# The second expert weight in two transfers, and the second product half by half of the inner units

## The chip, the cores and the metric

The kernel runs on one core of one Trainium2 chip. The metric is the device time of one execution in microseconds (us); lower is better. Engines are called as in the profile: PE (matmul), PEld (its weight loads), DVE (vector), ACT (scalar), POOL (which here issues the indexed transfers) and SP (which issues the plain ones).

## The reference

Four batches of 5056 tokens with 256 channels go through an attention over channels; its 20224 output rows go to one of 8 experts each. The core of it, shortened:

```
qn = q / (norm(q, axis=1) + 1e-6)          # q, k, v: 4 x 5056 x 256
kn = k / (norm(k, axis=1) + 1e-6)
a  = softmax(kn^T @ qn / tau)              # 4 x 256 x 256
x  = (v @ a).reshape(20224, 256)
e_idx  = argmax(x @ w_gate)                # one of 8 experts per row
gate_w = softmax(x @ w_gate)[e_idx];  eom = sigmoid(x @ w_output_gate)
for e in range(8):
    h  = relu(x[e_idx == e] @ w1[e])       # 256 -> 1024 inner units
    ye = h @ w2[e]                         # 1024 -> 256
    out[e_idx == e] = gate_w * eom[:, e] * ye
```

## The kernel before

**Stages.** The attention comes first: the products of k and q over all tokens (`gram`), then per batch v times a (`mix`), with the choice of the expert beside it (`route`), which scatters each token's row by expert into a buffer in DRAM, `xs_d`. The expert stage (`blocks`) starts while the last of that still runs, and fills the span from then on.

**Units.** The sorted tokens are worked off as 90 units. Units 0 to 53 have 256 tokens, that is two row tiles of 128 (`nt` is 2); from unit 54 on, units of 256 and of 128 tokens alternate. `FIRST` holds the first unit of each expert in the full part: 0, 7, 13, 20, 26, 33, 39 and 46.

**Numbers in two pieces.** x, h and both weights are kept as a sum of two fp16 numbers, hi and lo, and every product is three matmuls: hi by hi, hi by lo, lo by hi. `h_part` (L1011 to L1013) makes a quarter of the inner units, 12 matmuls, and ACT (L1015) and DVE (L1016) turn it into the hi and lo of `hb`. `y_part` (L1035 to L1037) makes a quarter of the second product. It has two row tiles t and two halves of the inner units fh, and takes tile 0 over the first half, tile 0 over the second, then tile 1 likewise: `t, fh = (part // 2, part % 2)`. ACT then scales y to `yo` (L1041), and POOL scatters `yo` to the output rows (L1048).

**Weights.** A weight is read as fp32 (`raw`), and `split` scales it by its size: ACT squares it (L348), DVE adds the sums up in `wtot` (L353), PE adds them over the partitions (`w_ps`, L354), and DVE takes the scale from it. Then ACT makes the hi (L369) and DVE the lo (L370), and SP writes both to `wsc` in DRAM (`keep`, L378). Each weight has two slots in SBUF, `wbuf`, and units take them in turn (`at_of`). Before a unit, POOL reads its weight from `wsc` into the slot (`fetch_w`, L904): 128 rows of 8 KB, found by an index per row from the table `wi`. Where the slot already holds that expert, the index lies out of bounds, and the transfer moves nothing. Units before the seventh use a weight that was split in place.

**x.** A unit's tokens come into `xg`, by POOL (L920) for units 20 to 68, else by SP. ACT (L985) and DVE (L986) make `xr` of them, hi and lo, and SP's transposing transfers (L990) turn this into `xt`. `xr` has two buffers, so that ACT waits with an `xr` for the transposes that still read the buffer.

**Order.** `blocks` writes iteration g as: fetch the first weight of the coming unit, the second weight of unit g, x some units ahead; store unit g-2; then four steps, each with a part of h of unit g and a part of y of unit g-1, and in between `prepare` for later x and the next steps of `split`. Each engine then works through its own list in a fixed order that a scheduler makes of this, by its own estimate of times; an instruction that waits holds up all that stands behind it on its engine. PE's list thus has h of a unit mixed with y of the one before, and now and then a `w_ps`. A transfer into a slot waits until PE has done with what the slot held: the first weight for h of two units before, the second for y of two units before.

## Time and profile before

| | |
|---|---|
| runs of the kernel | 1199.91, 1201.35 and 1203.97 us, median 1201.35 us |
| the profiled execution | 1198.02 us in all, of it 1196.3 us span |
| first matmuls on a fetched second weight | at 417 us |
| transfers issued by POOL | L904 into wbuf x166, L666 into xs_d x160, L1048 to the output x162, L920 into xg x49 |
| queue of POOL's transfers | 79.73 MB; its packets took 22.3% of the 16 DMA engines' span |
| queue of SP's transfers | 126.58 MB; 37.4% |

The profile is one execution, with times from the start of its span. In a timeline a row gives start, duration, engine, line, operation, tiles and, in brackets, the time for which the engine stood idle before it and what released it. A row of a group of instructions gives count, total busy time, mean ns of one, idle time before them and what ended most of it. A row of a window gives its length, then the busy time of PE, PEld, DVE, ACT and POOL with counts, the granted clock of PE, the busy share of the 16 DMA engines, and GB/s. "DMA wbuf<-wsc,wi" as a releaser means that a weight's transfer landed. In the names of tiles, `wbuf<-wsc,wi` stands for both weights.

### The profile page before, as it was taken

The page shows a single profiled execution, that of the slowest core. Times are in us where ns is not written, and L with a number is a line of the kernel's source. Part 1 is how long each engine was busy: PE and PEld are TensorE (multiplying, and loading weights), DVE is VectorE, ACT ScalarE, POOL GpSimd, SP SyncE. Part 2 cuts the span into 40 slices and gives each one's busy share as a digit, 9 for nine tenths or more (in the row PEclk, how much of TensorE's full clock was granted, in tenths as well). Part 3 has the DMA queues.
Part 4 walks back from the last instruction along what each step waited for, and adds up shares of the span by engine and source line. Part 5 has one row for each costly group of instructions (what it writes and reads, how often), then busy time and mean ns, then how long its engine had stood idle before and what let it go on. Part 6 is the DMA issues. An engine that isn't in the chain of part 4 may idle for free.

```text
span 1196.3 us, 27750 instructions
## 1 busy us (share of the span) xinstructions
PE 1170.8 (98%) x10412; PEld 1060.2 (89%) x10412; DVE 711.5 (59%) x2123; ACT 623.4 (52%) x1233; POOL 572.7 (48%) x561
## 2 busy tenths in 40 slices
PE   8999999999899999999999999999999999999998
PEld 7889899999788888888888888788889999999997
DVE  6666757658795755656565656554444555555551
ACT  5676757657745655546555555433333444444442
POOL 0004574757576334555544545444455644444443
PEclk9999999999999999999999999999999999999999
DMA  8986687857679964666655545732326442337643
GB/s 298 327 300 225 225 285 252 299 171 248 213 233 310 239 166 135 152 152 152 141 154 144 143 118 159 206 71 71 78 69 178 114 80 70 78 78 212 180 114 132
DMA packets 174882, 208.54 MB, mean 174 GB/s; under 512 B 120936, under 2 KB 124526, under 8 KB 169752
## 3 DMA queue, kind: packets, MB, share of 16 engines
q1 hardware_dynamic: 130312, 126.58, 37.4%
q0 software_dynamic: 43312, 79.73, 22.3%
q8 instruction: 84, 1.38, 0.5%
q10 hardware_dynamic: 1120, 0.42, 0.1%
q14 instruction: 54, 0.44, 0.1%
HBM read 275.55 MB, written 61.41 MB: 282 GB/s over the span
## 4 chain that ended last, share of the span: by engine, by line
PE 67%; issue 14%; POOL 8%; DMA 6%; ACT 2%; DVE 2%; SPq 1%; POOLq 0%; ACTq 0%; DVEq 0%
PE s_ps L444 9%; PE h_ps L1011 8%; PE h_ps L1013 8%; PE h_ps L1012 8%; PE y_ps L1037 8%; PE y_ps L1035 8%; PE y_ps L1036 8%; POOL out_dram L1048 4%; POOL wbuf L904 3%; PE x_ps L588 3%; PE x_ps L590 3%; PE x_ps L589 3%; PE vt_ps L558 2%; DMA qk<-in_k_dram 2%; DMA xt<-xr 1%
## 5 line engine op out<-in xcount | busy, mean ns | idle before, releaser
L1016 DVE SCALAR_TENSOR_TENSOR hb<-h_ps,hb 128x512 f16<-128x512 f32 (+1 forms) x360 | 228.0, 637 | 314.2 <-ACT hb L1015 314.0
L1015 ACT ACTIVATE hb<-h_ps 128x512 f16<-128x512 f32 (+1 forms) x360 | 197.2, 552 | 343.1 <-PE h_ps L1013 342.6
L1011 PE MATMUL h_ps<-xt,wbuf 128*128 128x256 f16 (+1 forms) x1440 | 366.6, 262 | 2.9 <-ACT st L591 2.9
L1013 PE MATMUL h_ps<-xt,wbuf 128*128 128x256 f16 (+1 forms) x1440 | 366.7, 262 | 0.0
L1012 PE MATMUL h_ps<-xt,wbuf 128*128 128x256 f16 (+1 forms) x1440 | 366.6, 262 | 0.0
L1035 PE MATMUL y_ps<-wbuf,hb 128*128 128x256 f16 x1296 | 353.3, 273 | 3.6 <-DMA wbuf<-wsc,wi 3.1
L1037 PE MATMUL y_ps<-wbuf,hb 128*128 128x256 f16 x1296 | 353.3, 273 | 0.3 <-DVE hb L1016 0.3
L1036 PE MATMUL y_ps<-wbuf,hb 128*128 128x256 f16 x1296 | 353.3, 273 | 0.0
L904 POOL DMA_INDIRECT wbuf<-wsc,wi x166 | 171.3, 1032 | 220.2 <-PE h_ps L1013 166.4
L666 POOL DMA_INDIRECT xs_d<-st,r_si x160 | 174.3, 1089 | 180.2 <-ACT st L591 96.1
L1048 POOL DMA_INDIRECT out_dram<-yo,b_id x162 | 169.9, 1049 | 64.4 <-issue 42.1
L1011 PEld LDWEIGHTS <-wbuf 128*128 128x128 f16 x1440 | 141.1, 98 | 15.7 <-issue 1.6
L1012 PEld LDWEIGHTS <-wbuf 128*128 128x128 f16 x1440 | 141.2, 98 | 15.3 <-issue 1.5
L444 PE MATMUL s_ps<-qk 128*128 128x256 f32 x640 | 149.4, 384 | 4.9 <-DMA qk<-in_q_dram 3.9
L1013 PEld LDWEIGHTS <-wbuf 128*128 128x128 f16 x1440 | 141.2, 98 | 13.5
L1036 PEld LDWEIGHTS <-hb 128*128 128x128 f16 x1296 | 126.8, 98 | 17.2 <-issue 3.4
L1037 PEld LDWEIGHTS <-hb 128*128 128x128 f16 x1296 | 126.8, 98 | 15.5 <-DVE hb L1016 0.8
L1035 PEld LDWEIGHTS <-hb 128*128 128x128 f16 x1296 | 126.8, 98 | 14.9 <-ACT hb L1015 1.1
L444 PEld LDWEIGHTS s_ps<-qk 128*128 128x128 f32 x640 | 119.0, 192 | 20.6 <-DMA qk<-in_k_dram 3.9
L920 POOL DMA_INDIRECT xg<-xs_d,gi x49 | 50.7, 1034 | 145.8 <-DVE xr L986 143.0
L406 DVE TENSOR_TENSOR acc<-acc,sq 128x1024 f32<-128x1024 f32 x76 | 93.1, 1225 | 45.8 <-ACT sq L405 39.9
L405 ACT ACTIVATE sq<-qk 128x1024 f32<-128x1024 f32 x76 | 80.4, 1060 | 53.3 <-DMA qk<-in_k_dram 47.3
(195 smaller groups left out, 1493.2 us busy)
## 6 DMA issues: line engine op xcount, KB each, us to landing
qk<-in_q_dram SPq DMA_DIRECT2D x75, 256.0 KB
qk<-in_k_dram SPq DMA_DIRECT2D x75, 256.0 KB
v<-in_v_dram SPq DMA_DIRECT2D x32, 512.0 KB
raw<-in_moe_w_dram SPq DMA_DIRECT2D x16, 1024.0 KB
xg<-xs_d SPq DMA_DIRECT2D x30, 272.0 KB
wsc<-whi SPq DMA_DIRECT2D x14, 512.0 KB
wsc<-wlo SPq DMA_DIRECT2D x14, 512.0 KB
v<-in_v_dram SPq DMA_DIRECT2D x8, 480.0 KB
```

Of the source, the lines that this page charges most:

```text
L444: nc.tensor.matmul(s_ps[:, c, :], kt[:, 1, t, c * P : (c + 1) * P], qt[:, 0, t, :], start=st == 0 and t0 == 0 and t == 0 and c == 0 and n ...
L666: ins = nc.gpsimd.indirect_dma_start(out=xs_d[:, :], out_offset=bass.IndirectOffsetOnAxis(ap=si[:np_, t : t + 1], axis=0), in_=st[:np_, t, ...
L904: nc.gpsimd.indirect_dma_start(out=wbuf[half][:, at_of(u), :], out_offset=None, in_=wsc[half][:end, :], in_offset=bass.IndirectOffsetOnAxi ...
L1011: nc.tensor.matmul(hp, w1s[:, 0, c, fs], xh, start=fi == 0 and c == 0, stop=False, **KWM)
L1012: nc.tensor.matmul(hp, w1s[:, 0, c, fs], xl, start=False, stop=False, **KWM)
L1013: main(PE=nc.tensor.matmul(hp, w1s[:, 1, c, fs], xh, start=False, stop=fin, **KWM))
L1015: main(ACT=nc.scalar.activation(hh, h_ps[:, :, :w], AF.Relu))
L1016: ins = nc.vector.scalar_tensor_tensor(out=hb[:, 1, 2 * fp : 2 * fp + 2, :w], in0=h_ps[:, :, :w], scalar=0.0, in1=hh, op0=ALU.max, op1=ALU ...
L1035: nc.tensor.matmul(y_ps[:, t, :], hb[:, 0, f, tsl], w2s[:, 0, f, :], start=st, stop=False, **KWM)
L1036: nc.tensor.matmul(y_ps[:, t, :], hb[:, 0, f, tsl], w2s[:, 1, f, :], start=False, stop=False, **KWM)
L1037: main(PE=nc.tensor.matmul(y_ps[:, t, :], hb[:, 1, f, tsl], w2s[:, 0, f, :], start=False, stop=fin, **KWM))
L1048: ins = nc.gpsimd.indirect_dma_start(out=out[:, :], out_offset=bass.IndirectOffsetOnAxis(ap=un["id"][:, t : t + 1], axis=0), in_=un["yo"][ ...
```

## The change

The second weight is laid out by halves of the inner units, in `wbuf` and in `wsc`: the half first, then hi and lo. It comes in two transfers of 128 rows of 4 KB, each with an index table of its own (`wi2`). `y_part` takes both row tiles over the first half (parts 0 and 1), then both over the second. The first half of the next unit's second weight is fetched after the second of the four steps of an iteration, the second half at the head of the next iteration, where the whole stood.

```diff
+    def by_pieces(a):
+        return a.rearrange("p (h a x) -> p h a x", h=2, a=2)
...
     def keep():
         with behind("SP"):
             for n, part in enumerate((hi, lo)):
-                nc.sync.dma_start(wsc[half][rows, n * HW1 : (n + 1) * HW1], part)
+                if half == 1:
+                    nc.sync.dma_start(by_pieces(wsc[1][rows, :])[:, :, n, :], part)
+                else:
+                    nc.sync.dma_start(wsc[half][rows, n * HW1 : (n + 1) * HW1], part)
...
+    wi2 = cst.tile([P, 2, NUNIT], I32, name="wi2")
...
         nc.vector.scalar_tensor_tensor(
-            out=wi[:, a:b], in0=ok, scalar=float(BIG), in1=row, op0=ALU.mult, op1=ALU.add
-        )
+            out=row, in0=ok, scalar=float(BIG), in1=row, op0=ALU.mult, op1=ALU.add
+        )
+        nc.vector.tensor_copy(wi[:, a:b], row)
+        for n in range(2):
+            nc.vector.tensor_scalar(
+                out=wi2[:, n, a:b], in0=row, scalar1=2.0, scalar2=float(n), op0=ALU.mult, op1=ALU.add
+            )
...
+    def fetch_w2(u, n):
+        if u < FIRST[1]:
+            return
+        end = 2 * (units[u]["top"] + 1) * P
+        nc.gpsimd.indirect_dma_start(
+            out=wbuf[1][:, at_of(u), 2 * n * (HW1 // 2) : 2 * (n + 1) * (HW1 // 2)],
+            out_offset=None,
+            in_=wsc[1].rearrange("r (n w) -> (r n) w", n=2)[:end, :],
+            in_offset=bass.IndirectOffsetOnAxis(ap=units[u]["wi2"][:, n, :], axis=0),
...
-        t, fh = (part // 2, part % 2) if nt == 2 else (0, part)
+        t, fh = (part % 2, part // 2) if nt == 2 else (0, part)
...
-            adv("w2", lambda u: fetch_w(1, u), g + NW - 1)
+            adv("w2a", lambda u: fetch_w2(u, 0), g + NW - 1)
+            adv("w2b", lambda u: fetch_w2(u, 1), g + NW - 1)
...
+                if fp == 1:
+                    adv("w2a", lambda u: fetch_w2(u, 0), g + NW)
```

In the engines' lists the first place is PE's, where unit 7's first y part begins (y of L1035 to L1037, h of L1011 to L1013; in the changed kernel these are L1069 to L1071 and L1044 to L1046). Before:

```order
L1013 MATMUL h_ps<-xt,wbuf_161 128x256
L1011 LDWEIGHTS wbuf_161
L1011 MATMUL h_ps<-xt,wbuf_161 128x256
L1035 LDWEIGHTS hb
L1035 MATMUL y_ps<-wbuf_162,hb 128x256
```

And in the changed kernel:

```order
L1045 MATMUL h_ps<-xt,wbuf_161 128x256
L1046 LDWEIGHTS wbuf_161
L1046 MATMUL h_ps<-xt,wbuf_161 128x256
L1069 LDWEIGHTS hb
L1069 MATMUL y_ps<-wbuf_162,hb 128x256
```

Before, y begins behind the first matmul of a triple, the seventh matmul of unit 8's second h part; now it begins behind the last of a triple, which ends the first h part, and is seven matmuls earlier in the list.

The second place is POOL's list among the units of two sizes (`wbuf_161` is the first weight, `wbuf_162` the second, `wi_169` the table `wi2`). Before, two units:

```order
L904 DMA wbuf_161<-wsc_85,wi 128x4096
L904 DMA wbuf_162<-wsc_86,wi 128x4096
L1048 DMA out_dram<-yo,b_id 20224x256 x2
L904 DMA wbuf_161<-wsc_85,wi 128x4096
L904 DMA wbuf_162<-wsc_86,wi 128x4096
L1048 DMA out_dram<-yo,b_id 20224x256
```

And in the changed kernel:

```order
L937 DMA wbuf_162<-wsc_86,wi_169 128x2048
L922 DMA wbuf_161<-wsc_85,wi 128x4096
L937 DMA wbuf_162<-wsc_86,wi_169 128x2048
L1082 DMA out_dram<-yo,b_id 20224x256
L937 DMA wbuf_162<-wsc_86,wi_169 128x2048
L922 DMA wbuf_161<-wsc_85,wi 128x4096
L937 DMA wbuf_162<-wsc_86,wi_169 128x2048
L1082 DMA out_dram<-yo,b_id 20224x256 x2
```

Per unit there is one transfer more, the first half of the second weight; it stands ahead of the next first weight, behind the stores.

The third place is on PE at a `w_ps` between units 28 and 29, here with the numbers of the buffers. Before (`y_ps_9389` is y of unit 27, `h_ps_9540` begins h of unit 29):

```order
L1037 LDWEIGHTS hb_9216
L1037 MATMUL y_ps_9389<-wbuf1_162,hb_9216 128x256
L354 LDWEIGHTS onesb_94
L354 MATMUL w_ps_9510<-wtot_9511,onesb_94 128x1
L1011 LDWEIGHTS wbuf0_161
L1011 MATMUL h_ps_9540<-xt_9129,wbuf0_161 128x256
```

And in the changed kernel (`y_ps_9631` is y of unit 28, `h_ps_9616` begins h of unit 29):

```order
L1069 LDWEIGHTS hb_9446
L1069 MATMUL y_ps_9631<-wbuf1_162,hb_9446 128x256
L363 LDWEIGHTS onesb_94
L363 MATMUL w_ps_9586<-wtot_9587,onesb_94 128x1
L1044 LDWEIGHTS wbuf0_161
L1044 MATMUL h_ps_9616<-xt_9199,wbuf0_161 128x256
```

`w_ps` now stands behind 22 matmuls of unit 28's y, which stood behind it before; the `w_ps` between units 34 and 35 has moved in the same way. On DVE nothing has moved at the `w_ps` behind unit 39: there, in both lists, two `xr`, two pieces of `hb` and then `wtot` follow each other, and on PE `w_ps` stands behind the same 22 matmuls of unit 39.

More of the change, by code (lines that the diff above doesn't have):

```diff
@@ L328, in split @@
         rows = slice(r * P, (r + 1) * P)
-        if r == 0:
+        if r == 0 and half == 1:
+            hi, lo = (by_pieces(wbuf[1][:, 0, :])[:, :, n, :] for n in range(2))
+        elif r == 0:
             hi, lo = (wbuf[half][:, 0, n * HW1 : (n + 1) * HW1] for n in range(2))
@@ L365, in split @@
         else:
-            src, dh, dl = raw, hi, lo
-            cuts = [(slice(None), slice(i * HW1 // 2, (i + 1) * HW1 // 2)) for i in range(2)]
+            src, dh, dl = raw.rearrange("p (h x) -> p h x", h=2), hi, lo
+            cuts = [(slice(None), i) for i in range(2)]
         for i, a in enumerate(cuts):
@@ L851, in add @@
                 units.append(
[L852 removed]
+                    dict(nt=nt, gi=gi[:, u : u + 1], wi=wi[:, u : u + 1], wi2=wi2[:, :, u : u + 1], top=max(r for r in range(E) if FIRST[r] <= u))
                 )
@@ L904, in fetch_w @@
         nc.gpsimd.indirect_dma_start(
-            out=wbuf[half][:, at_of(u), :],
+            out=wbuf[0][:, at_of(u), :],
             out_offset=None,
-            in_=wsc[half][:end, :],
+            in_=wsc[0][:end, :],
             in_offset=bass.IndirectOffsetOnAxis(ap=units[u]["wi"], axis=0),
+            bounds_check=end - 1,
+            oob_is_err=False,
+        )
[3 more added lines that the diff above has]
+        end = 2 * (units[u]["top"] + 1) * P
+        assert 2 * len(prepped) * P >= end
+        nc.gpsimd.indirect_dma_start(
[3 more added lines that the diff above has]
+            in_offset=bass.IndirectOffsetOnAxis(ap=units[u]["wi2"][:, n, :], axis=0),
             bounds_check=end - 1,
@@ L1034, in y_part @@
             fin = part == 3 and f == FC - 1
[L1035 to L1037 removed]
+            wh, wl = (w2s[:, a, f // (FC // 2), f % (FC // 2), :] for a in range(2))
+            nc.tensor.matmul(y_ps[:, t, :], hb[:, 0, f, tsl], wh, start=st, stop=False, **KWM)
+            nc.tensor.matmul(y_ps[:, t, :], hb[:, 0, f, tsl], wl, start=False, stop=False, **KWM)
+            main(PE=nc.tensor.matmul(y_ps[:, t, :], hb[:, 1, f, tsl], wh, start=False, stop=fin, **KWM))
         if part == 3:
```

17 lines of the change are left out of this document (8 added, 9 removed).

## The prediction

> **What bounds the kernel now.** First the page's head, to see which engine fills the span; then PE over the stretch in which the two products run; then PE's waits, which name all that can be won there.
>
> ```profile
> span 1196.3 us, 27750 instructions
> PE 1170.8 (98%) x10412; PEld 1060.2 (89%) x10412; DVE 711.5 (59%) x2123; ACT 623.4 (52%) x1233; POOL 572.7 (48%) x561
> PEclk9999999999999999999999999999999999999999
> ```
>
> PE is busy for 98% of the span, at the full granted clock in all 40 slices: no clock to win, and 25 us without work. One window takes in the units from the first fetched second weight on (span, then busy time of PE, PEld, DVE, ACT, POOL, clock, DMA share, GB/s); below it are PE's waits.
>
> ```profile
> 417.00:1176.00 759.00, 756.06 (x7324) 681.28 (x7324) 414.60 (x1259) 348.27 (x683) 366.85 (x355) 1.00 0.50 130
> ...
> PE y_ps L1035 <- DMA wbuf<-wsc,wi: 3.1, 2, 1.7
> PE w_ps L354 <- DVE wtot L353: 2.5, 3, 2.1
> PE y_ps L1035 <- ACT hb L1015: 0.5, 1, 0.5
> PE y_ps L1037 <- DVE hb L1016: 0.3, 1, 0.3
> ```
>
> In 759 us PE stands still for 759.00 - 756.06 = 2.94 us, and its matmul count does not change. In the whole span it waits for a second weight twice, 3.1 us together, once just ahead of this window and once in it. So the change cannot win much: first the ceiling, place by place. A wait is counted here as a gap beyond the cadence of matmuls, 0.11 us in the rows below (417.00 to 417.11 and so on).
>
> **Unit 7, the first weight wait** (PE's timeline; the number before the arrow is idle time; the windows as above; the last row is the piece of the chain that the load makes).
>
> ```profile
> 415.37 0.27 PE L1011 MATMUL h_ps<-xt,wbuf 128*128 128x256 f16 x1
> 417.00 0.27 PE L1035 MATMUL y_ps<-wbuf,hb 128*128 128x256 f16 x1 [1.36 <-DMA wbuf<-wsc,wi]
> 417.11 0.27 PE L1036 MATMUL y_ps<-wbuf,hb 128*128 128x256 f16 x1
> ...
> 412.00:414.50 2.50, 2.50 (x26) 2.24 (x24) 2.50 (x7) 2.50 (x3) 1.98 (x2) 1.00 1.14 397
> 414.50:417.00 2.50, 1.14 (x11) 0.88 (x9) 2.50 (x6) 1.34 (x4) 2.10 (x2) 1.00 0.71 263
> ...
> 408.50 8.46 DMA wbuf<-wsc,wi
> ```
>
> The next matmul would have been due at 415.37 + 0.11 = 415.48; it starts at 417.00, 1.52 us late. The load was issued at 408.50 and is in use 8.46 us later. Now two things change. The first half stands alone at the head of the queue, and the new order puts unit 7's first y part 7 matmuls earlier (before the second h part, where it stood in the middle of it), so PE asks at 415.48 - 7 x 0.11 = 414.71. When is half of the weight there? From 412.0 to 417.0 the DMA engines moved 2.5 x 397 + 2.5 x 263 = 1650 KB, of which the load's 128 rows of 8 KB are 1049 KB. If its packets went ahead of the others, 524 KB take 524/397 = 1.3 us, to 413.3; if all shared evenly, 825 KB take 2.1 us, to 414.1. I add up to 0.8 us until PE may use it, an estimate: by the same even pace the bytes end near 417. So 413.3 to 414.9, against 414.71: PE waits 0 to 0.2 us. **Term 1: -1.4 us**, bounds 0 (the half lands no earlier than the whole) and -1.52. The second half is asked for by the third part only, at least 36 matmuls (two parts of y and one of h, 3.9 us) after the first.
>
> A rule of the Trainium skill speaks against this, in "DMA: Bandwidth & Descriptors", section "Anatomy of one DMA — SWDGE (gpsimd) path": a transfer costs about 2.0 us that do not depend on its size, and bytes at 436 GB/s. By it the whole load would take 4.4 us and a half 3.2 us, estimates; the first half would come only 1.2 us sooner, at 415.8, and the term would be -0.4 us. The trace has 8.46 us for the whole, so the fixed part is not what sets it here.
>
> What gates the issue at 408.50 is the weight's way into DRAM: the load reads what SP writes here.
>
> ```profile
> 402.20 0.42 SPq L378 DMA_DIRECT2D wsc<-wlo  x1
> ```
>
> The change writes it in pieces of 2 KB instead of 4 KB (the wsc rows of the second weight are interleaved by halves). From 402.20 to 408.50 the write and the release take 6.3 us; no row has 2 KB pieces. If it gets 1.4 us slower, term 1 is gone; if faster, PE has nothing left to win. I take no change, the nearest row being this same write.
>
> **Unit 39, the second weight wait.** PE, then ACT and DVE, then the transfers ahead of them.
>
> ```profile
> 751.24 0.27 PE L1037 MATMUL y_ps<-wbuf,hb 128*128 128x256 f16 x1
> 753.23 0.27 PE L1035 MATMUL y_ps<-wbuf,hb 128*128 128x256 f16 x1 [1.72 <-DMA wbuf<-wsc,wi]
> 755.90 0.28 PE L1035 MATMUL y_ps<-wbuf,hb 128*128 128x256 f16 x1 [0.54 <-ACT hb L1015]
> 756.62 0.28 PE L1037 MATMUL y_ps<-wbuf,hb 128*128 128x256 f16 x1 [0.34 <-DVE hb L1016]
> 756.85 0.17 PE L354 MATMUL w_ps<-wtot,onesb 128*128 128x1 bf16 x1
> ...
> 754.46 0.91 ACT L985 ACTIVATE xr<-xg,b_sx 128x256 f16<-128x256 f32 x2 [6.24 <-DMA xt<-xr]
> ...
> 755.00 0.88 DVE L986 SCALAR_TENSOR_TENSOR xr<-xg,b_sx,xr 128x256 f16<-128x256 f32 x2 [6.05 <-ACT xr L985]
> 755.88 0.69 DVE L1016 SCALAR_TENSOR_TENSOR hb<-h_ps,hb 128x512 f16<-128x512 f32 x1
> 756.48 0.15 DVE L353 TENSOR_TENSOR wtot<-wss 128x1 bf16<-128x1 f32 x1
> ...
> 742.18 12.03 DMA xt<-xr
> ...
> 742.80 1.00 POOL L904 DMA_INDIRECT wbuf<-wsc,wi  x1 [0.30 <-issue]
> ```
>
> PE loses 753.23 - 751.35 = 1.88 us for the weight, then about 0.7 and 0.5 us for hb beyond the cadence: 3.1 us. The load was issued at 742.80. In the changed kernel its first half goes out as soon as unit 37's first two y parts are over, 24 matmuls and what lies between them sooner, so the weight will be there. But see what is late next. Behind 22 matmuls of unit 39 (12 + 10) stands w_ps, in both orders, and it reads wtot. wtot is DVE's third work behind xr, xr waits for ACT's xr, and ACT's xr waits for the transposes that end 742.18 + 12.03 = 754.21, because they still read the buffer that xr writes. Nothing of the change stands in that chain. So w_ps starts at 756.85 again, and PE, 22 x 0.11 = 2.4 us of matmuls after 751.35, waits for it from 753.8: the wait for the weight becomes a wait for wtot of about 3.0 us. **Term 2: -0.1 us.** Can the transposes land earlier? They share the DMA engines with the loads:
>
> ```profile
> 736.00:740.00 4.00, 4.00 (x40) 3.58 (x38) 3.84 (x14) 1.75 (x4) 2.00 (x2) 1.00 0.76 154
> 746.00:753.00 7.00, 5.51 (x51) 4.80 (x49) 2.55 (x11) 0.60 (x1) 0.44 (x1) 1.00 0.93 347
> ...
> 756.15 1.04 POOL L920 DMA_INDIRECT xg<-xs_d,gi  x1 [9.71 <-DVE xr L986]
> ```
>
> The first half of unit 39 moves out of the full stretch (0.93) into a freer one (0.76): 524 KB, at 347 GB/s 1.5 us less. But POOL is free for the 9.7 us before 756.15, and after unit 38's first two y parts the first half of unit 40 goes out in just that time and takes the room again. So I take no shift. Bounds: all 3.1 us won, if the transposes land 3 us earlier; 1.0 us lost, if the half of unit 40 holds them up by about as much (half of those 524 KB in their way).
>
> **The rest.** At two places w_ps waits for wtot by itself:
>
> ```profile
> 635.05 0.27 PE L1037 MATMUL y_ps<-wbuf,hb 128*128 128x256 f16 x1
> 635.49 0.18 PE L354 MATMUL w_ps<-wtot,onesb 128*128 128x1 bf16 x1 [0.17 <-DVE wtot L353]
> ...
> 698.83 0.18 PE L354 MATMUL w_ps<-wtot,onesb 128*128 128x1 bf16 x1 [0.17 <-DVE wtot L353]
> ...
> 365.69 0.18 PE L354 MATMUL w_ps<-wtot,onesb 128*128 128x1 bf16 x1 [2.14 <-DVE wtot L353]
> ...
> 364.84 0.69 DVE L1016 SCALAR_TENSOR_TENSOR hb<-h_ps,hb 128x512 f16<-128x512 f32 x1 [4.56 <-ACT hb L1015]
> ```
>
> 635.49 - 635.05 - 0.11 = 0.33 us each (the second like the first); the new order puts both 22 matmuls, 2.4 us, later on PE. **Term 3: -0.7 us**, bounds 0 and -0.7. At 365.69 three more matmuls stand ahead of w_ps (-0.3), but one yo of some 0.4 us stands ahead of hb on ACT, on whose end the DVE row waits (+0.4): **term 4: +0.1 us**, bounds -0.3 and +0.4. The added DVE work, three small operations in the weight tables, lies in the 4.56 us in which DVE waits for that hb: nothing; without that cover, about as much as three rows like wtot, 0.5 us.
>
> The price that recurs is POOL's:
>
> ```profile
> L904 POOL DMA_INDIRECT wbuf<-wsc,wi x166 | 171.3, 1032 | 220.2 <-PE h_ps L1013 166.4
> ...
> 1085.04 1.04 POOL L904 DMA_INDIRECT wbuf<-wsc,wi  x1 [3.56 <-PE h_ps L1013]
> 1092.30 1.01 POOL L904 DMA_INDIRECT wbuf<-wsc,wi  x1 [3.57 <-PE h_ps L1013]
> ...
> 1093.18 0.27 PE L1011 MATMUL h_ps<-xt,wbuf 128*128 128x256 f16 x1
> ```
>
> Half of 166, 83 more issues of 1.032 us, with 0.3 us between issues: some 110 us on POOL. Each goes out in the middle of a unit, when POOL waits anyway: 3.56 us ahead of the row at 1085.04, against 1.3 us. In POOL's order it stands ahead of the next xg and first weight, but what it waits for (the second y part) is over before what they wait for. Bytes are the same. **Nothing**; without this cover, see the slower rival. Sum: -1.4 - 0.1 - 0.7 + 0.1 = **-2.1 us**. The profiled execution took 1198.02 us (its span and 1.7 us around it), so 1195.9; the runs' median is 1201.35, 3.3 us above it, so 1199.3.
>
> **Rivals.**
> *Both weight waits vanish whole.* The transposes land 3 us earlier, wtot with them: -1.5 - 3.1 - 0.7 = -5.3 us, 1192.7 profiled, 1196.1 by the median (-0.44%). For it: the DMA engines are full until the weight lands, and what is ahead of the transposes gets less. Against: unit 40's half takes the room. Chance 0.2.
> *Slower: first weights land late among the pairs.* There the first weight goes out at 1085.04 and h uses it at 1093.18, 8.1 us later, while the loads above took 8.46 and 753.23 - 742.80 = 10.4 us. PE does not wait there now, so loads there are quicker or skipped. From the point at which a first weight lands more than 8.1 us after its issue, PE waits: 0.4 to 2.3 us by these two. Such loads come with a change of expert, seven changes times two slots, 14 at most; at half a microsecond each that is +7 us, 1205 profiled, 1208 by the median. For it: a third transfer shares the queue, and an issue of 1.3 us may stand ahead. Against: the half goes out sooner, and DMA is busy 0.50 of the window. Chance 0.1.
> *The halves are no sooner.* If the first half waits for all of the earlier y, or lands with the second, terms 1 and 2 are nothing, and 3 and 4 leave -0.6: 1197.4 profiled, 1200.8. For it: the release is seen on no row of before. Chance 0.1.
>
> **How the numbers follow.** Forecast 0.6, rivals 0.2, 0.1, 0.1. A measurement of this kernel tells apart some 0.3%, 3.6 us. Forecast and third rival lie inside, of the first rival most lies beyond, and single runs spread from 1199.91 to 1203.97, so I say faster 0.22, same 0.67, slower 0.11. The range has to reach the first rival, 1196.1 with 1 us for spread, and on the other side the bounds of terms 1, 2 and 4 (0, +1.0, +0.4: 1202.8 with no term 3): 1195.0 to 1203.3; the slower rival stays out.
>
> **What will show it.** Right: no wait of y for wbuf near 415; near 753 the same hole, but ahead of w_ps, put down to wtot, w_ps within 0.5 us of 756.85 less what was won before; no wait at the w_ps of 635 and 699; POOL busy for some 85 us more, PE as long as before. Wrong: y still waiting for wbuf (the halves land late), h waiting for wbuf between 900 and 1176 (slower rival), or transposes that end a microsecond or more earlier (first rival).

## The result, and the profile after

The changed kernel is **slower**, by 1.4%. Beside each other on one chip, its median is 1221.92 us (six runs, 1210.05 to 1223.93) and that of the kernel before 1202.66 us (six runs, 1197.74 to 1214.76): a ratio of 1.0142, with a 95% interval of 1.0103 to 1.018. The prediction said 1199.3 us, in a range from 1195.0 to 1203.3. The profiled execution took 1220.71 us, of it 1219.0 us span, which is 22.7 us more than the span before.

The head of the page after, then two lines of PE's waits (waited for: us in total, times, longest):

```profile
span 1219.0 us, 28028 instructions
PE 1176.1 (96%) x10412; PEld 1065.0 (87%) x10412; DVE 715.3 (59%) x2129; ACT 624.0 (51%) x1233; POOL 660.4 (54%) x644
PEclk9999999999899999999999999899999999999998
```

```profile
PE w_ps L363 <- DVE wtot L362: 10.4, 3, 9.8
PE y_ps L1069 <- DMA wbuf<-wsc,wi: 3.1, 1, 3.1
```

The matmuls are the same in number. POOL is busy for 660.4 - 572.7 = 87.7 us more with 83 more transfers, as forecast (85). Three slices show a granted clock below 0.9: around 305 to 335 us, where unit 0 begins, at unit 39 and at the end (a 9 stands for 0.9 or more, so it doesn't say that the clock was full). Where a weight was waited for twice, it is now waited for once, for as long; and a wait for `wtot` of 9.8 us has come up. These waits are not 22.7 us, so the rest has to be looked for where the waits of PE don't reach. Placing the same matmuls of the two timelines side by side, unit by unit, gives this ledger:

| stretch | lost (us) | forecast (us) |
|---|---|---|
| up to unit 6 | 2.1 | +0.1 (the `w_ps` of 365.69 us) |
| unit 7, first half of its weight | 3.1 | -1.4 |
| the two `w_ps` of 635 and 699 us | -0.8 | -0.7 |
| unit 39 | 8.3 | -0.1 |
| behind the last matmul | 9.95 | none |
| sum | 22.7 | -2.1 |

**Up to unit 6.** Of the 2.1 us, 1.55 stand ahead of unit 0's first matmul. Then the profiles part twice, by PE's clock. Both have a hole ahead of unit 0, of 3.12 us after and 2.94 before; behind it PE works at 0.50 after and at 1.00 before, and 2.4 us are lost. At the first `w_ps` that waited for `wtot` (365.69 us before) it is the other way round: before, 3.41 us at 0.50 follow the wait of 2.14 us; after, the waits there are 1.00 (for `hb`) and 0.40 us and the clock stays full, so that 2.2 us are won. By the next `w_ps` 0.4 are lost again. The windows, after and then before:

```profile
328.50:334.20 5.70, 5.69 (x34) 4.84 (x34) 2.33 (x9) 2.47 (x9) 4.20 (x5) 0.50 0.29 104
```

```profile
327.00:329.40 2.40, 2.40 (x22) 2.27 (x21) 1.15 (x7) 1.88 (x8) 1.79 (x3) 1.00 0.28 101
366.39:369.80 3.41, 3.41 (x19) 2.43 (x17) 2.20 (x3) 3.41 (x4) 2.54 (x3) 0.50 1.07 264
```

**The end.** The stretch from the last matmul to the end of the span, in windows, after and then before (length, busy time of PE, PEld, DVE, ACT, POOL, clock, DMA share, GB/s):

```profile
1203.40:1219.00 15.60, 0.00 (x0) 0.00 (x0) 0.00 (x0) 0.47 (x1) 1.40 (x2) 0.65 0.04 14
```

```profile
1190.60:1196.30 5.70, 0.04 (x1) 0.00 (x0) 0.00 (x0) 0.47 (x1) 1.44 (x2) 0.96 0.12 41
```

Nothing works in it, and what stands there issues no work, so neither busy times nor waits name it. The view of one source line names it: the last instructions of POOL's own sequencer (shortest/median/longest in ns, then the first and the last start in us). After and before:

```profile
L1178 POOLq INC_SWDGE_SEM  x1: 2071/2071/2071, 1208.3 to 1208.3; - x1
...
L1205 POOLq DRAIN  x3: 51/103/7745, 1210.4 to 1218.7; - x3
```

```profile
L1141 POOLq INC_SWDGE_SEM  x1: 411/411/411, 1194.1 to 1194.1; - x1
...
L1168 POOLq DRAIN  x3: 51/103/967, 1194.5 to 1196.0; - x3
```

One drain takes 7.745 us instead of 0.967, and the instruction ahead of it 2.071 instead of 0.411: 6.78 + 1.66 = 8.4 of the 9.95 us. The first stands at the test whether a rest of units is left, the second at the program's end; neither does work of the kernel. The other 1.5 us stand ahead of both: the first of them starts 4.9 us behind the last matmul instead of 3.4. They vary by themselves: in five other profiles with the same count of transfers and all halves early, or all but one (`e1_again`, `e3_head`, `e9_but40`, `e15_but39`, `e18_change`) the end takes 13.75 us or 13.76 instead of 15.62.

**Unit 39.** In order, each from its own view after: PE's timeline, ACT's, DVE's, the piece of the chain of waits that the transposes make, and POOL's issues ahead of and during them.

```profile
768.11 0.18 PE L363 MATMUL w_ps<-wtot,onesb 128*128 128x1 bf16 x1 [9.79 <-DVE wtot L362]
...
768.38 0.42 PE L1045 MATMUL h_ps<-xt,wbuf 128*128 128x256 f16 x1
768.59 0.42 PE L1046 MATMUL h_ps<-xt,wbuf 128*128 128x256 f16 x1
```

```profile
765.88 0.91 ACT L1018 ACTIVATE xr<-xg,b_sx 128x256 f16<-128x256 f32 x2 [13.25 <-DMA xt<-xr]
...
767.90 0.15 DVE L362 TENSOR_TENSOR wtot<-wss 128x1 bf16<-128x1 f32 x1
```

```profile
746.60 19.02 DMA xt<-xr
```

```profile
742.13 1.02 POOL L937 DMA_INDIRECT wbuf<-wsc,wi  x1 [0.30 <-issue]
...
745.68 1.00 POOL L922 DMA_INDIRECT wbuf<-wsc,wi  x1 [0.30 <-PE y_ps L1071]
746.99 1.00 POOL L937 DMA_INDIRECT wbuf<-wsc,wi  x1 [0.30 <-PE h_ps L1046]
...
750.96 1.03 POOL L937 DMA_INDIRECT wbuf<-wsc,wi  x1 [0.33 <-PE y_ps L1071]
```

The chain is the one that the prediction followed, from the transposes over ACT's `xr` and DVE's `xr` and `hb` to `wtot` and `w_ps`. Only its first link has another length: 19.02 us where it had 12.03. The four issues are unit 39's first half, unit 40's first weight, unit 39's second half and unit 40's first half. Windows of the trace after show what the transposes met (first over all of their 19.02 us, then a part of them), and what the hole did to PE's clock; below, apart, is the window over the transposes before:

```profile
746.60:765.62 19.02, 11.72 (x108) 10.27 (x105) 3.76 (x12) 1.79 (x3) 4.14 (x5) 0.88 0.92 211
752.00:754.00 2.00, 2.00 (x20) 1.80 (x19) 1.14 (x4) 0.60 (x1) 0.00 (x0) 1.00 0.17 59
758.30:768.10 9.80, 0.02 (x1) 0.00 (x0) 1.64 (x4) 2.12 (x5) 0.53 (x1) 0.63 0.54 164
768.20:771.10 2.90, 2.90 (x15) 2.09 (x16) 1.58 (x5) 2.32 (x3) 2.29 (x3) 0.50 1.21 172
```

```profile
742.18:754.21 12.03, 10.31 (x95) 9.10 (x93) 3.62 (x12) 1.79 (x3) 3.35 (x4) 1.00 0.88 282
```

While the transposes ran, 19.02 x 211 = 4013 KB were moved, against 12.03 x 282 = 3392 KB before. The 621 KB more account for 2.2 us at 282 GB/s; the other 4.8 of the 7.0 us are a lower rate, and in the part from 752 to 754 the engines moved just 59 GB/s, with transposes still to land. The packets of the trace show what stood there: fourteen of POOL's, of 4352 bytes each, the size in which x comes into `xg` (64 of them are a unit's 272 KB), began between 748.87 and 750.99, took 2.1 to 5.7 us and ended between 753.1 and 754.5; ten more (nine of x, one of a first weight) began from 754.01 on and ended together at 757.4. The median packet of x takes 0.2 us in this stretch. In the last window, behind the hole, PE works at 0.50 of its clock: a matmul every 0.21 us (768.38, 768.59) instead of 0.11, which is 14 matmuls by 0.1 = 1.4 us. With the 7.0 us by which the transposes take longer, that makes the 8.3 within a tenth.

**Unit 7.** PE's timeline after, the load's piece of the chain, and windows before and behind the hole:

```profile
420.05 0.37 PE L1069 MATMUL y_ps<-wbuf,hb 128*128 128x256 f16 x1 [3.07 <-DMA wbuf<-wsc,wi]
```

```profile
408.91 11.10 DMA wbuf<-wsc,wi
```

```profile
416.00:418.00 2.00, 0.98 (x9) 0.72 (x8) 2.00 (x5) 1.95 (x5) 1.69 (x2) 1.00 1.03 168
...
420.00:421.00 1.00, 0.95 (x5) 0.69 (x5) 0.55 (x2) 0.83 (x2) 0.19 (x1) 0.50 1.04 362
421.00:422.00 1.00, 1.00 (x7) 0.67 (x6) 0.59 (x2) 0.07 (x1) 1.00 (x1) 0.50 0.51 190
```

Half the weight took 11.10 us, where the whole had taken 8.46. PE begins y 420.05 - 417.00 = 3.05 us later than before, of which 2.1 were lost earlier; it has then done 7 matmuls of h less (0.8), and 14 or so matmuls run at half the clock (1.4): 3.1 us in all.

### The profile page after: what moved, and what is told of

Its sections match the earlier page's. It is cut to its first block, busy times and chain, and to the rows that moved or that the text cites. A ratio compares the mean times of both kernels' runs of the same rounds, so it can differ in the third digit from the quotient of the medians.

```text
span 1219.0 us, 28028 instructions
## 1 busy us (share of the span) xinstructions
PE 1176.1 (96%) x10412; PEld 1065.0 (87%) x10412; DVE 715.3 (59%) x2129; ACT 624.0 (51%) x1233; POOL 660.4 (54%) x644
## 3 DMA queue, kind: packets, MB, share of 16 engines
q8 instruction: 84, 1.38, 0.5%
## 4 chain that ended last, share of the span: by engine, by line
PE 83%; DMA 7%; issue 3%; ACT 2%; POOL 2%; DVE 1%; POOLq 0%; SPq 0%; ACTq 0%; DVEq 0%
PE h_ps L1044 10%; PE h_ps L1045 10%; PE h_ps L1046 10%; PE y_ps L1069 10%; PE y_ps L1071 10%; PE y_ps L1070 10%; PE s_ps L456 9%; PE x_ps L600 3%; PE x_ps L602 3%; PE x_ps L601 3%; PE vt_ps L570 2%; DMA xt<-xr 2%; DMA qk<-in_k_dram 2%; POOL xs_d L678 1%; DMA xs_d<-st,r_si 1%
## 5 line engine op out<-in xcount | busy, mean ns | idle before, releaser
L1044 PE MATMUL h_ps<-xt,wbuf 128*128 128x256 f16 (+1 forms) x1440 | 367.3, 263 | 3.1 <-ACT st L603 3.1
L1046 PE MATMUL h_ps<-xt,wbuf 128*128 128x256 f16 (+1 forms) x1440 | 367.1, 263 | 0.0
L1069 PE MATMUL y_ps<-wbuf,hb 128*128 128x256 f16 x1296 | 353.8, 273 | 4.1 <-DMA wbuf<-wsc,wi 3.1
L1071 PE MATMUL y_ps<-wbuf,hb 128*128 128x256 f16 x1296 | 353.9, 273 | 0.0
L678 POOL DMA_INDIRECT xs_d<-st,r_si x160 | 177.1, 1107 | 178.7 <-ACT st L603 97.6
L937 POOL DMA_INDIRECT wbuf<-wsc,wi x166 | 172.2, 1037 | 89.8 <-PE y_ps L1071 58.3
L1044 PEld LDWEIGHTS <-wbuf 128*128 128x128 f16 x1440 | 141.3, 98 | 16.3 <-DMA xt<-xr 1.9
L1046 PEld LDWEIGHTS <-wbuf 128*128 128x128 f16 x1440 | 141.4, 98 | 13.6
L922 POOL DMA_INDIRECT wbuf<-wsc,wi x83 | 85.0, 1024 | 106.7 <-PE h_ps L1046 96.6
L1069 PEld LDWEIGHTS <-hb 128*128 128x128 f16 x1296 | 127.0, 98 | 15.3 <-ACT hb L1048 1.3
L1071 PEld LDWEIGHTS <-hb 128*128 128x128 f16 x1296 | 127.0, 98 | 15.1 <-DVE hb L1049 0.2
```

The source lines that it names most:

```text
L678: ins = nc.gpsimd.indirect_dma_start(out=xs_d[:, :], out_offset=bass.IndirectOffsetOnAxis(ap=si[:np_, t : t + 1], axis=0), in_=st[:np_, t, ...
L937: nc.gpsimd.indirect_dma_start(out=wbuf[1][:, at_of(u), 2 * n * (HW1 // 2) : 2 * (n + 1) * (HW1 // 2)], out_offset=None, in_=wsc[1].rearra ...
L1044: nc.tensor.matmul(hp, w1s[:, 0, c, fs], xh, start=fi == 0 and c == 0, stop=False, **KWM)
L1046: main(PE=nc.tensor.matmul(hp, w1s[:, 1, c, fs], xh, start=False, stop=fin, **KWM))
L1069: nc.tensor.matmul(y_ps[:, t, :], hb[:, 0, f, tsl], wh, start=st, stop=False, **KWM)
L1071: main(PE=nc.tensor.matmul(y_ps[:, t, :], hb[:, 1, f, tsl], wh, start=False, stop=fin, **KWM))
```

## The experiments

Two theories stood against each other. **Places:** the halves, sent out earlier, meet the transposes, and the two holes are the loss. **Count:** 83 more transfers cost by themselves, at the end or between. Ratios are to the kernel before on the same chip. The chips differ: before took 1203 to 1205 us on the chip of the result and on that of `e5` to `e8`, but 1285 to 1294 us on the four others, where PE loses, in the profiles taken there, many small waits that the profile puts to "issue", with no releaser. So most verdicts below rest on a place in the trace, not on the total.

### Which part is it: the order, the early half, or the count?

**The change once more**, on another chip.

> The changed kernel once more, unchanged. Theory A (the early half of unit 40's weight runs beside the transposes and holds them up): the same picture, w_ps behind unit 39 waits 8 to 11 us for wtot, the transposes of about 747 take 17 to 20 us, ratio to before 1.010 to 1.018. Theory D (the long transposes and the long end were an accident of one execution): the wait falls to 3 us or the end stretch (last matmul to end of span, 15.9 us against 5.9 before) to 6 us, and single times spread by over 8 us.

1317.55 against 1294.4 us, ratio 1.020 (1.0138 to 1.0262). PE's timeline and the transposes in the chain:

```profile
844.99 0.19 PE L363 MATMUL w_ps<-wtot,onesb 128*128 128x1 bf16 x1 [10.93 <-DVE wtot L362]
```

```profile
825.01 17.48 DMA xt<-xr
```

The wait of unit 39 and the long transposes come again on a chip that is slower throughout. Unit 7 waits 1.9 us here.

**The new order of y alone**, in the kernel before.

```diff
-        t, fh = (part // 2, part % 2) if nt == 2 else (0, part)
+        t, fh = (part % 2, part // 2) if nt == 2 else (0, part)
```

> The kernel before with the new order of y's parts alone: both row tiles over the first half of the inner units, then over the second; the second weight whole as before. Theories A and B (issue count): nothing changes, ratio 0.997 to 1.003, the first weight wait still 1.4 us, w_ps at 757. Theory C (the order itself costs): slower by 0.5% or more, with y waiting for hb somewhere.

1299.4 us, ratio 1.0037 (1.0003 to 1.0072). PE waits 4.0 us for unit 39's weight, nowhere long for `wtot`, and the end stretch is 5.56 us. The order is not the loss.

**Both halves called at the head of the iteration**, nothing after the second step.

```diff
-                if fp == 1:
-                    adv("w2a", lambda u: fetch_w2(u, 0), g + NW)
```

> The changed kernel with both halves fetched at the head of the iteration, nothing early: as many issues as the change, bytes of unit 40 no longer beside the transposes. Theory A: the transposes near 745 take 12 us again, w_ps behind unit 39 waits 3 us or less, -8 us against the change; if the long end comes from the number of issues (theory B) it stays at 14 to 16 us and the ratio to before is about 1.008; if not, 1.000 to 1.003. Theory B alone (more transfers as such slow the transposes): w_ps waits 8 us or more here too, ratio 1.010 to 1.018.

1315.54 us, ratio 1.0159 (1.0099 to 1.022). The scheduler brought POOL's transfers into the same order as in the change, the first halves early, so this undid nothing: `w_ps` waits 9.5 us and the end takes 13.75 us, as with the change. It is a third profile of that order. Where a call stands in the code does not say where the transfer goes.

**83 empty transfers in the kernel before**: all their indices lie out of bounds, so each costs an issue and moves nothing.

```diff
+                if fp == 1 and FIRST[1] <= g + 1 < min(len(units), z):
+                    none_i = sm.tile([P, 1], I32, tag="none_i", name="none_i")
+                    nc.vector.tensor_scalar(
+                        out=none_i, in0=units[g]["id"][:, 0:1], scalar1=0.0, scalar2=float(BIG), op0=ALU.mult, op1=ALU.add
+                    )
+                    nc.gpsimd.indirect_dma_start(
+                        out=none_o[:, :],
...
```

> The kernel before with one more indexed transfer per unit from unit 7 on, all of its indices out of bounds, so that it moves nothing, in POOL's list where the change has the first half (and one small DVE operation for its index). Theory B: the end stretch grows to 14 to 16 us and the ratio is 1.006 or more; if the transposes suffer from the number of transfers too, 1.010 or more. Theory A: the middle stays as before, w_ps behind unit 39 near 757 with no wait beyond 3 us; ratio 0.998 to 1.004 if the long end isn't from the count of issues.

1341.18 us, ratio 1.038 (1.0306 to 1.0455). There is no long wait for `wtot` (the longest is 0.6 us), but the end takes 14.06 us, with the drain at 7745 ns to the nanosecond of the change. So the count alone brings the end; the halves are not needed for it. PE's "issue" waits add up to 66 us, against 43 to 54 in the three runs above, so the total is no measure of the price.

### The parts apart, on a chip as fast as that of the result

**Both halves late**, one right behind the other at the head of the iteration.

```diff
+    def fetch_both(u):
+        b = fetch_w2(u, 1)
+        if b is not None:
+            with tc.issue_after(b.ins):
+                fetch_w2(u, 0)
...
-            adv("w2a", lambda u: fetch_w2(u, 0), g + NW - 1)
-            adv("w2b", lambda u: fetch_w2(u, 1), g + NW - 1)
+            adv("w2", fetch_both, g + NW - 1)
...
-                if fp == 1:
-                    adv("w2a", lambda u: fetch_w2(u, 0), g + NW)
```

> The changed kernel with both halves issued next to each other, the second half and then the first, when the whole of the earlier y is over: as many transfers as the change, but no half of unit 40 before the w_ps behind unit 39. Theory A (unit 40's early half, beside the transposes, makes them long): transposes 10 to 13 us at that place, w_ps waits 0 to 3 us for wtot; end stretch 14 to 16 us as in the change, ratio to before about 1.007. Rival (any second weight in two transfers of 4 KB rows makes them long): w_ps waits 8 us or more again, ratio 1.012 or more.

1208.04 against 1204.67 us, ratio 1.0051 (1.0009 to 1.0093). PE's timeline at unit 39, the transposes, and the end:

```profile
752.26 0.27 PE L1075 MATMUL y_ps<-wbuf,hb 128*128 128x256 f16 x1 [0.57 <-DMA wbuf<-wsc,wi]
...
755.63 0.18 PE L363 MATMUL w_ps<-wtot,onesb 128*128 128x1 bf16 x1 [0.81 <-DVE wtot L362]
```

```profile
742.63 10.50 DMA xt<-xr
```

```profile
L1208 POOLq DRAIN  x3: 103/199/7745, 1195.7 to 1204.2; - x3
```

The transposes are short again, and neither weight nor `wtot` holds PE for a microsecond. Unit 7 does not wait at all. What is left is the end, 14.22 us. Against the change's 1.0142 about two thirds of the loss are gone.

**Everything but the second transfer**: the layout by halves, the write in pieces of 2 KB, the new order, one transfer of 8 KB rows.

```diff
-            adv("w2a", lambda u: fetch_w2(u, 0), g + NW - 1)
-            adv("w2b", lambda u: fetch_w2(u, 1), g + NW - 1)
+            adv("w2", fetch_w2, g + NW - 1)
...
-                if fp == 1:
-                    adv("w2a", lambda u: fetch_w2(u, 0), g + NW)
```

> The changed kernel's layout (halves outermost, SP writes of 2 KB pieces) and order of y, but the second weight in one transfer of 8 KB rows: as many transfers as before. Theory A and the count of transfers: as before, ratio 0.997 to 1.005, end stretch 5 to 6 us, no w_ps wait beyond 3 us. Rival (the 2 KB pieces or the layout cost): the load of the first second weight is issued later than 6.3 us after its write, or the transposes get long here too, ratio 1.008 or more.

1204.37 us, ratio 0.9995 (0.9952 to 1.0038); end 5.67 us, transposes 11.92 us. No loss and no gain: layout, order and the smaller write pieces cost nothing that can be told.

**41 empty transfers instead of 83**, in the kernel before (580 transfers on POOL's queue instead of 539).

```diff
-                if fp == 1 and FIRST[1] <= g + 1 < min(len(units), z):
+                if fp == 1 and 49 <= g + 1 < min(len(units), z):
```

> The kernel before with the empty transfer for units 49 to 89 only: 41 more transfers in place of 83. If the long end grows with the number of transfers, the end stretch is about half-way, 9 to 11 us; if it is a step that some count sets off, it is 5 to 6 or 14 to 16 us. Ratio 1.003 to 1.02, from the end stretch and what the empty transfers cost elsewhere.

1210.31 us, ratio 1.0046 (1.0005 to 1.0086), 5.6 us by the medians; the end takes 10.68 us instead of 5.67, 5.0 of them. Its drain:

```profile
L1182 POOLq DRAIN  x3: 51/103/4315, 1199.6 to 1204.5; - x3
```

Half the transfers bring half the longer drain: (4315 - 967)/41 = 82 ns each, and (7745 - 967)/83 = 82 ns. On a chip without the small waits, no cost is seen but the end, of which the two instructions make 4.2 us.

**The kernel before once more.**

> The kernel before, for its profile on this chip, to stand beside the others: ratio 0.998 to 1.002, end stretch 5 to 6 us, no w_ps wait beyond 3 us behind unit 39.

1204.69 us, ratio 0.9989 (0.9955 to 1.0023). Its profiled execution was the longest of the ten, of 1217.05 us; it is of use for one window:

```profile
759.00:763.00 4.00, 4.00 (x39) 3.57 (x38) 1.70 (x9) 0.60 (x1) 0.00 (x0) 1.00 0.14 27
```

The standstill of the transfers, 27 GB/s with a weight and transposes under way, is there without the change too. PE waited 7.84 us for the weight of unit 39 in it, and 3.77 us at unit 7. The packets show the same too: fifteen rows of a weight (8192 bytes) began between 756.78 and 759.29, took 4.8 to 7.3 us and ended together at 764. So the change does not make a thing that was never there; the question is what makes it regular.

### Which half meets the transposes, and does the count alone make the end?

**The change, but unit 40's half late.** The prediction had named that half as what "takes the room".

```diff
+    def ahead_of(u):
+        return u != 40
+
+    def fetch_w2a(u):
+        if ahead_of(u):
+            fetch_w2(u, 0)
+
+    def fetch_w2b(u):
+        b = fetch_w2(u, 1)
+        if b is not None and not ahead_of(u):
+            with tc.issue_after(b.ins):
+                fetch_w2(u, 0)
```

> The change with one transfer of 83 moved: unit 40's first half is issued behind its second half, like in e5_late; all others stay early. Theory A (this one transfer, beside the transposes that the next xr waits for, makes the long wait): w_ps behind unit 39 waits 0 to 3 us instead of 9.8, the transposes take 10 to 13 us; end stretch 14 to 16 us; ratio to before 1.004 to 1.009. Rival (any early half does it, unit 39's too): the wait stays 7 to 11 us, ratio 1.010 or more.

1312.01 against 1291.83 us, ratio 1.0156 (1.0093 to 1.022). PE's timeline and the transposes:

```profile
832.82 0.19 PE L363 MATMUL w_ps<-wtot,onesb 128*128 128x1 bf16 x1 [8.53 <-DVE wtot L362]
```

```profile
816.03 14.29 DMA xt<-xr
```

The wait stays. Unit 40's half is not it.

**All late, but unit 40's half early.**

```diff
-        return u != 40
+        return u == 40
```

> The reverse: all halves late as in e5_late, only unit 40's first half early. Theory A: the long wait of w_ps comes back, 7 to 11 us, transposes 16 to 20 us, ratio to before 1.010 to 1.016. Rival: it stays away, ratio 1.003 to 1.008.

1368.54 us, ratio 1.0559 (1.0487 to 1.063). At unit 39 the longest wait for `wtot` is 1.2 us and that for the weight 2.2, with transposes of 12.17 us: the counterpart of the run before. "Issue" waits add up to 89 us in it, against 39 in the run before, so the total says nothing of the place.

**Fewer transfers than before**: the kernel before, with x of units 55 to 68 by SP (525 on POOL's queue).

```diff
-    BY_POOL = range(20, 69)
+    BY_POOL = range(20, 55)
```

> The kernel before with x of units 55 to 68 read by SP in place of POOL: 14 POOL transfers fewer. From 539, 580 and 622 transfers the final drain on POOL took 0.97, 4.32 and 7.75 us, 0.082 us for each more. If that holds below 539 too, the drain is 0 to 0.1 us at 525 and the end stretch 4.2 to 4.8 us instead of 5.7; if 539 is already its floor, 5.5 to 5.8 us. Ratio 0.995 to 1.003, as the moved reads should cost nothing.

1295.55 us, ratio 1.0051 (1.001 to 1.0091), and the end takes 14.74 us:

```profile
L1141 POOLq INC_SWDGE_SEM  x1: 2241/2241/2241, 1285.5 to 1285.5; - x1
...
L1168 POOLq DRAIN  x3: 51/103/8480, 1287.8 to 1296.8; - x3
```

14 transfers fewer, and the drain is 8480 ns instead of 967. So it does not grow with the count without end: it climbs and falls back, and the kernel before stood just behind such a fall.

**A selection**: the layout of `e6_layout`, halves at unit 7 only, and the last `w_ps` a step earlier.

```diff
-        yield from pause(WAITW)
+        yield from pause(0 if (half, r) == (1, E - 1) else WAITW)
...
+        if u == FIRST[1]:
+            fetch_half(u, 0)
+            return fetch_half(u, 1)
```

> What is left of the change where it is worth something: the new layout and order of y, the second weight in two transfers for unit 7 alone and in one elsewhere, and the last w_ps one step earlier, so that its wtot stands ahead of the xr that waits for the transposes. 540 transfers: end stretch 5.7 us. By the waits that go: 1.5 us at unit 7, 0 to 3 us at unit 39; ratio to before 0.995 to 0.999. If PE waits for hb of unit 39 or the whole second weight instead, 0.998 to 1.002.

1308.2 us, ratio 1.0107 (1.0061 to 1.0152). `w_ps` no longer waits at unit 39, but the transposes there took 19.22 us, and h of the next units waited 5.7 us for its weight and 3.9 us for the scale. With one early `w_ps` the wait is only moved, and the standstill can come without unit 39's early half.

### The cause of the long transposes, and a way around both losses

**The change with 28 empty transfers among units 60 to 87** (650 in all), to get behind the next fall of the drain.

```diff
+                if fp == 1 and 60 <= g + 1 < 88:
...
+                    nc.gpsimd.indirect_dma_start(
+                        out=none_o[:, :],
...
```

> The change with 28 empty transfers more on POOL, at units 60 to 87, 650 in all. If the final drain is a sawtooth over the number of transfers (period some 105 to 115), it is over its edge here: drain 0.5 to 1.8 us in place of 7.75, end stretch 5 to 7 us in place of 14 to 16, so more transfers make the kernel some 8 us faster: ratio to before 1.003 to 1.010. If the drain grows with the count, it takes about 10 us, end stretch 16 to 18 us, ratio 1.015 to 1.020.

1314.51 against 1287.8 us, ratio 1.0229 (1.0162 to 1.0296). The end is 6.53 us:

```profile
L1192 POOLq INC_SWDGE_SEM  x1: 510/510/510, 1302.5 to 1302.5; - x1
...
L1219 POOLq DRAIN  x3: 51/103/1375, 1303.1 to 1305.0; - x3
```

More transfers than the change, and a drain of 1375 ns: it has fallen again. But the kernel is no faster for it: "issue" waits take 47 us, and `w_ps` still waits 7.1 us.

**Both halves late, with the same 28 empty ones.**

```diff
-            adv("w2a", lambda u: fetch_w2(u, 0), g + NW - 1)
-            adv("w2b", lambda u: fetch_w2(u, 1), g + NW - 1)
+            adv("w2", fetch_both, g + NW - 1)
```

> e5_late with the same 28 empty transfers: both halves late, 650 transfers. By the sawtooth the end stretch falls from 14.2 to 5 to 7 us and the ratio from 1.005 to 0.996 to 1.000; by growth 1.006 to 1.009.

1364.09 us, ratio 1.0586 (1.0505 to 1.0667). Both places are good (end 5.96 us; at unit 39 no wait for `wtot` and 2.4 us for the weight), and "issue" waits take 83 us.

**The change, but unit 39's first half late**, and its counterpart, **all late but unit 39's first half**. Edits of `ahead_of` alone, against `e9_but40`:

```diff
-        return u != 40
+        return u != 39
```

> The change with only unit 39's first half late (behind its second half), all others early, unit 40's too. If unit 39's early half causes the long wait: w_ps waits 0 to 3 us, the transposes take 10 to 13 us, ratio about 1.006. If not: 7 us or more, ratio 1.010 or more.

```diff
-        return u != 40
+        return u == 39
```

> All halves late, only unit 39's first half early. If that one transfer causes the long wait: w_ps waits 7 to 11 us, transposes 16 to 20 us, ratio 1.010 to 1.014. If not: 0 to 3 us, ratio about 1.005.

The first: 1298.67 us, ratio 1.010 (1.0038 to 1.0162); no wait for `wtot` there, but 2.31 us for the weight, and the chain goes through a load of 9.88 us:

```profile
818.67 9.88 DMA wbuf<-wsc,wi
```

The second: 1350.36 us, ratio 1.0517 (1.0452 to 1.0583); PE's timeline and the chain:

```profile
850.70 0.19 PE L363 MATMUL w_ps<-wtot,onesb 128*128 128x1 bf16 x1 [9.31 <-DVE wtot L362]
```

```profile
832.50 15.70 DMA xt<-xr
```

Of 83 early halves, the one of unit 39 brings the wait when it alone is early, and takes it away when it alone is late. The total of the second is far above the 1.010 to 1.014 that was expected, as with the two others on these chips whose halves are all late, or all but one (`e10_only40`, `e14_late650`).

**Unit 39 late, with the 28 empty ones**, beside **the change** (the last kernel differs from it by a comment only).

```diff
+        return u != 39
...
+                if fp == 1 and 60 <= g + 1 < 88:
```

> The change with unit 39's first half late and 28 empty transfers more (650): both causes taken away. If they are the whole loss: end stretch 5.5 to 7 us, w_ps behind unit 39 waits 0 to 3 us, ratio to before 0.998 to 1.004. If something of the change costs all along: 1.006 or more.

> The change, unchanged, beside e17_both: ratio 1.012 to 1.020, w_ps waits 7 to 11 us, end stretch 13.5 to 16 us; 16 us or more above e17_both if the two causes are the whole loss.

1313.14 us, ratio 1.021 (1.0129 to 1.0291), and 1303.26 us, ratio 1.017 (1.0103 to 1.0238), against 1284.71. At unit 39, the first and then the second:

```profile
833.24 0.18 PE L363 MATMUL w_ps<-wtot,onesb 128*128 128x1 bf16 x1 [1.16 <-DVE wtot L362]
```

```profile
841.55 0.18 PE L363 MATMUL w_ps<-wtot,onesb 128*128 128x1 bf16 x1 [9.89 <-DVE wtot L362]
```

The first is 9 to 10 us ahead by units 43 to 53, and ends 6.55 us behind its last matmul instead of 13.75; then it loses some 29 us in units 54 to 85, where its empty transfers stand. Its "issue" waits add up to 58 us against 39; their first line among PE's waits:

```profile
PE h_ps L1060 <- issue: 16.2, 27, 1.7
```

So each of the two losses can be taken away, and on this chip the means costs more than it gives. By the totals the expectation failed: the first was to be 16 us or more faster than the second, and is 10 us slower. On the chip of the result this kernel was not run. No kernel came out faster than the one before; the best, `e6_layout`, is even with it.

## Why the prediction was wrong, step by step

**Two steps made the forecast fall.** They were wrong as mechanisms, not in size.

*"Half of 166, 83 more issues ... Nothing."* POOL's idle time did cover the issues, as said, and the 87.7 us showed nowhere among the units. What the step left out is that a count of transfers has a price at the end of the program, where nothing covers it: of the 9.95 us more behind the last matmul, 8.4. That it is the count was shown by empty transfers in the kernel before (the same 7745 ns with 83, 4315 ns with 41) and by a kernel with fewer of them and a longer drain. The page of before held a hint only in its last 5.7 us, in which PE does nothing; the prediction never looked at that stretch, since it went by PE's waits.

*Term 2, unit 39, -0.1 us with bounds of -3.1 and +1.0.* The exchange was right: the wait for the weight is gone, and `w_ps` waits for `wtot` in its place. The failed sentence is "Nothing of the change stands in that chain." The transposes stand in it, and they share the DMA engines with the half that the change moved: 19.02 us instead of 12.03. The bound of +1.0 shared bytes out evenly, as if the engines kept their rate; the mean fell from 282 to 211 GB/s. And the half named as the danger, unit 40's, was the wrong one: `e9_but40`, `e15_but39` and `e16_only39` show that unit 39's own first half does it. In all seven profiles of kernels that send it early, `w_ps` waits 7.1 to 10.9 us; of the thirteen that don't, eleven wait at that place for nothing longer than 4.0 us. The two others are `e8_before` and `e12_select`, which moved that `w_ps` itself. So the early half makes regular what else happens at times. The packets draw the same line: in each of the seven, 12 or more packets of POOL's queue stand for 2.1 to 8.3 us in the 26 us ahead of that `w_ps` and end in bunches, rows of x in the profile of the result and rows of a first weight (8192 bytes) in the six others; so do rows of a weight in `e8_before` and, around the moved `w_ps`, in `e12_select`; in the other eleven at most four packets there take over 2 us. The packets that stand are thus for the most part neither transposes nor rows of unit 39's half. Why they stand, and what the early half has to do with it, stays open. Nor is the length of the transposes the whole of the wait everywhere: in `e13_after650` they took 12.48 us, no longer than in kernels without the wait, and `w_ps` waited 7.1 us, for PE came to it 7.9 us behind their issue instead of 11.7.

The clock added to it. After the hole of 9.8 us PE ran at 0.50 for 2.9 us, another 1.4 us. The Trainium skill has this in "TensorE: Matmul & The Clock Gate", section "Part 1: The HAM clock gate": after an idle window of about 3.4 us the clock is halved, and about 3.4 us of steady work bring it back. The trace agrees in the length: in the profiles on the two fast chips half clock lasts 3.41, 6.83 or 10.24 us at a time, but for the end. It doesn't agree that it takes so long a hole: from unit 0 on, these six profiles have twelve holes of 2.1 to 3.8 us, and half clock followed on six of them (the shortest 2.14 us, before) and not on the six others (the longest 3.77 us, `e8_before`); it followed on all three longer ones (4.38, 7.84 and 9.79 us), and once came without such a hole (`e5_late`, 387 us). The prediction priced every wait at its own length and read "no clock to win" off slices whose 9 hides 3.41 us of half clock in the profile before.

*Term 1, unit 7, -1.4 us with bounds of 0 and -1.52.* PE did ask earlier, and the half was not there: 11.10 us from issue to use. In this profile the step that a half lands sooner than the whole, with "no earlier" as the worst, failed. Yet this wait varies by itself. In the eight profiles with unit 7's half early PE waits for it 0, 0, 0, 0.7, 0.9, 1.4, 1.9 and, in that of the result, 3.07 us; in the seven with one transfer 0, 0.8, 1.4, 2.1, 2.2, 2.4 and 3.8 us, where 1.4 and 3.8 are of one kernel (before and `e8_before`); in five with both halves late 0, 1.2, 2.1, 2.6 and 4.0 us. So the early half comes rather sooner than later, but not for sure; the profile of the result is the worst of eight. One profile can't size the term, and 3.1 us for it are not shown to be the change's. Nor are the 2.1 us ahead of unit 6.

*Term 3, -0.7 us*, held: neither `w_ps` has idle time ahead of it any more, and the stretch gained 0.8. *Term 4, +0.1 us with bounds of -0.3 and +0.4*, missed: that `w_ps` waits 0.40 us instead of 2.14, with 1.00 us for `hb` ahead of it, and without the half clock that followed before, the changed kernel wins 2.2 us there and keeps 1.8 of them at the next `w_ps`. The sum took a wait for its length only, and here the rest was the clock.

*The layout, the write in pieces of 2 KB, three small operations of DVE: nothing.* Held, by `e6_layout` (0.9995).

**The rivals.** Both waits vanish: no, though `e5_late` shows that halves sent late come close to that on a fast chip (no wait at unit 7, 0.57 and 0.81 us at unit 39). First weights late among the pairs: no, in the profile after no h waits for a weight; on the slower chips h does, once, for 4.7 us in `e3_head` and 2.7 in `e17_both`, but also for 1.9 in `e2_order`, which has no second transfer. The slower rival had the right suspect, 83 more transfers on a queue, and the wrong place. Halves no sooner: right at unit 7 in the profile of the result, where the half came even later, and wrong at unit 39, where no y waits for the weight any more.

## What to carry to other kernels

Count what closes a program, too: where a change adds transfers of one kind, look at the last microseconds behind the last work, in the view of the closing instructions, before calling added issues free. Before a transfer is moved ahead, list what is on the DMA engines at its new time, and treat a transfer on the critical chain beside it as one that may take half as long again, not as one that shares bytes evenly. A hole of two microseconds or more on PE can cost more than its length: half clock followed on half of those of 2.1 to 3.8 us, for 3.41 us or more, and even a slice that shows a 9 can hide it. Before a place is sized from one profile, look at how far the same wait varies over profiles of the same kernel.

## What the runs showed of the hardware

**The drain is a sawtooth.** The longest drain of POOL's sequencer at the end, by the number of indexed transfers that POOL issued: 525: 8.48 us; 539: 0.97; 540: 1.05 (`e12_select`); 580: 4.32; 622: 7.75 (ten profiles, all 7745 ns); 650: 1.38. That is 82 ns per transfer, from 539 to 540 as from 539 to 622, with a fall somewhere between 525 and 539 and again between 622 and 650; by the slope, 525 and 631 would stand alike, and 544 and 650, a period of some 106. The instruction ahead of it follows in the same shape at 20 ns each (2.24, 0.41, 0.43, 1.24, 2.07 and 0.50 to 0.51 us). What is counted there, and where a fall lies exactly, was not tried.

**Transfers that stand still.** While a weight's rows and transposes were under way, the DMA engines fell to 59 GB/s after the change and to 27 in `e8_before`, a kernel without it, where the mean over the transposes was 211 and, in the profile before, 282. With unit 39's half early the transposes took 12.48 to 19.02 us; in the other kernels whose chain shows them, 10.38 to 12.61, and 19.22 in `e12_select`. In these stretches a dozen or more row packets of POOL's queue stand for 2.1 to 8.3 us, and many of them end at the same moment (fourteen within 1.5 us after the change, fifteen within 0.2 us in `e8_before`).

**Chips differ by 7%** for one kernel (1203 and 1285 to 1294 us). On the slower ones PE has many waits with no releaser, most of them below 2 us, and they add up to 34 to 89 us; on the two fast ones the profiles have none. The three kernels with nearly all or all halves late on slow chips have 59 (`e16_only39`), 83 (`e14_late650`) and 89 us (`e10_only40`), and the worst totals; but `e17_both` has 58 us at a ratio of 1.021 against the 1.0517 of `e16_only39`, so these waits don't account for all of it. The one on a fast chip, `e5_late`, shows nothing of it. Why, stays open.
